# Paired PSUM tiles in the products and in-place column steps in a fused GEGLU and spectral-filter kernel

## The chip, the core and the metric

The kernel runs on one core of a Trainium2 chip. The metric is device microseconds (us) for one execution; the kernel before has a median of 1388.94 us over three runs (1387.86 to 1393.79).

The engines are named as the profile names them. PE is the matrix engine (PEld is its loading of weights), DVE the vector engine, ACT the scalar engine, POOL a fourth engine that here issues the DMAs that add into memory, and SP the engine that issues nearly all other DMAs. Each engine runs its own list of instructions strictly in the order in which the program wrote them. PSUM is the memory into which PE writes its sums, eight banks of 128 partitions by 512 numbers; SBUF is the memory from which the engines work. A program's buffers are *tiles*; the framework in which the kernel is written puts a semaphore wait in front of an instruction wherever a tile that it touches is still in use by another engine.

## The reference

```python
g = sigmoid((x * gate_w).sum(-1, keepdims=True))
a = irfft2(rfft2(x) * (w_r + 1j * w_i))          # over the 2048 x 576 plane
h = gelu_tanh(x @ w_gate) * (x @ w_up)           # 576 -> 4608
b = h @ w_down                                   # 4608 -> 576
out = g * a + (1 - g) * b                        # 2048 x 576, fp32
```

## The kernel before

**The GEGLU part** takes nearly all of PE's time. The 2048 tokens are four blocks of 512 (`TB`), the 4608 columns 36 tiles of 128. The first tiles are done directly (`chain`, L802). For the rest, two column tiles and two token blocks at a time are one *group* k, 0 to 33, and the four products of a group are made from seven by a Strassen–Winograd scheme (`products`, L1295). The seven products n = 0 to 6 carry the names a11, a12, s2, s3, s1, a22, s4. Each is made twice, once for the gate's columns (half s = 0) and once for the up-projection's (s = 1). A half is one call of `seven` (L1279): six matmuls of 128x512 (L1286) and one over 96 rows (L1288). Results pile up in PSUM. After n = 0 ACT copies each half into the accumulator of the other kind (`copy`, L235); after n = 2 and n = 3 it copies each half out to `xraw` in SBUF; after n = 4 and n = 6 DVE adds a half to what stands in `xraw` (`add`, L1328). Between the products stand eight calls of `down` a group (L891, twelve matmuls of 128x288), the down-projection of the group before. ACT moves each of their results to a staging tile (`stg<-pdn`, L923), and POOL adds it into memory by DMA (`yd<-stg`, L904).

PSUM before is split so that each half of a product has a tile of its own: `pgu` with two buffers, `px0` and `px1`, and `pdn` with two buffers of two banks each.

**The spectral part** (`spectral`) runs beside the groups: the rows' transforms, then 16 column steps (`columns`, L255) in which PE transforms blocks, DVE multiplies by the filter's weights and PE transforms back, then `inverse_tiles`, then the inverse of the rows in two parts (`inverse_rows`), which ends by adding its result into memory (`adds`). The column steps work on four groups of four tiles; a group needs a butterfly and twiddles (`four`, `tile_twiddles`) before its first step and again after its last. In between the operands of the second token half are made (`other_operands`) and, in group 15 (the *turn*), swapped in.

**The order of the work** is written out by the program. After each half product and each `down` comes a `gap`, in which the spectral part gets a credit of vector time that grows with PE's matmuls (RATE 1.08 against them) and writes pieces until the credit is spent. `at(n, f)` writes f some gaps later. STEP is the price of a column step in credit. So an instruction stands in its engine's queue where its gap put it, however late its inputs are. The queues of SP's DMAs have eight lanes; a DMA waits until its lane's previous one has landed.

## Time and profile before

| | |
|---|---|
| median of three runs | 1388.94 us (1387.86 to 1393.79) |
| the profiled execution | 1389.9 us, its span 1388.1 us |
| PE busy | 1330.7 us of the span, 7210 matmuls |
| DVE busy | 1150.5 us, 1814 instructions |
| ACT busy | 802.4 us, 1395 instructions |
| mean granted clock of PE | 0.983 |
| moved by DMA | 279.19 MB |

The span is what the profiler saw on the core, 1.8 us less than the execution. A page of the profile lists busy times; its slices cut the span into 40 equal pieces, where a digit is a tenth of the slice. The view of waits sums idle time of an engine by the instruction that ended it. The timeline lists instructions in order, with start and duration in us; a bracket gives the idle time just before and what released the engine. Successive matmuls overlap, so their starts are 0.23 us apart while each lasts 0.40. "x6" is six instructions in one row.

### The profile page before, as it was taken

How to read it: one execution, taken by the hardware profiler on the slowest of the kernel's cores; microseconds unless marked ns; L12 is line 12 of the kernel's file. 1: busy time of each engine (PE TensorE's matmuls, PEld its weight loads, DVE VectorE, ACT ScalarE, POOL GpSimd, SP SyncE). 2: the span in 40 equal slices, each digit the busy share in tenths (PEclk: the TensorE clock that was granted, in tenths of full speed). 3: DMA queues.
4: the chain of work that ended last, by engine and by line, in shares of the span. 5: the costliest groups of instructions: out<-in, count | busy, mean ns of one | idle time of the engine just before them, and what ended most of it. 6: DMA issues, size and time to landing. Idle time of an engine off the chain costs nothing. (4 is left out here: it accounts for less than half of the span.)

```text
span 1388.1 us, 21347 instructions
## 1 busy us (share of the span) xinstructions
PE 1330.7 (96%) x7210; PEld 1168.4 (84%) x7210; DVE 1150.5 (83%) x1814; ACT 802.4 (58%) x1395; POOL 274.8 (20%) x345
## 2 busy tenths in 40 slices
PE   9999999999999999796798989999999999999996
PEld 7878888888888888685787878888888888888896
DVE  7799999879989977664687787796999997899974
ACT  5575655655565556754575756665555556656541
POOL 0011111212111211111131122211211113311131
PEclk9999999999999999998899999999999999999999
DMA  9558888998877799899997979998877779977788
GB/s 345 197 138 181 175 182 175 236 260 188 183 135 135 135 248 306 239 254 291 253 265 191 263 164 256 247 270 233 172 134 135 133 134 207 180 141 132 129 181 222
DMA packets 184173, 279.19 MB, mean 201 GB/s; under 512 B 25920, under 2 KB 93568, under 8 KB 182144
## 3 DMA queue, kind: packets, MB, share of 16 engines
q0 software_dynamic: 47424, 91.51, 42.7%
q1 hardware_dynamic: 133184, 176.70, 40.5%
q10 hardware_dynamic: 3456, 9.62, 2.0%
q8 instruction: 57, 0.93, 0.3%
q14 instruction: 52, 0.43, 0.1%
HBM read 146.13 MB, written 129.20 MB: 198 GB/s over the span
## 5 line engine op out<-in xcount | busy, mean ns | idle before, releaser
L904 POOL DMA_DIRECT2D yd<-stg x264 | 228.4, 869 | 1044.4 <-ACT stg L923 973.3
L923 ACT ACTIVATE stg<-pdn,omg 128x576 f32<-128x576 f32 x276 | 204.3, 742 | 380.6 <-PE pdn L891 245.2
L891 PE MATMUL pdn<-dn,hb 128*128 128x288 f32 x1356 | 204.1, 298 | 13.0 <-ACT stg L923 12.9
L891 PEld LDWEIGHTS pdn<-dn,hb 128*128 128x128 f32 x1356 | 194.9, 190 | 23.4 <-ACT stg L923 14.9
L891 PE MATMUL pdn<-dn,ext 128*128 128x288 f32 x816 | 134.4, 301 | 22.4 <-ACT stg L923 14.3
L891 PEld LDWEIGHTS pdn<-dn,ext 128*128 128x128 f32 x816 | 125.6, 193 | 34.6 <-ACT stg L923 16.5
L1286 PE MATMUL pgu<-xhi,gub 128*128 128x512 f32 x480 | 152.5, 399 | 1.0 <-DVE gl L1311 1.0
L1286 PE MATMUL pgu<-til,gub 128*128 128x512 f32 x516 | 135.3, 398 | 7.0 <-ACT xraw L235 7.0
L891 PE MATMUL pdn<-dn,gub 128*128 128x288 f32 x816 | 132.2, 298 | 0.0
L235 ACT ACTIVATE gub<-low 128x512 fp32r<-128x512 f32 (+1 forms) x163 | 100.8, 620 | 31.3 <-DVE low L1257 17.6
L1286 PEld LDWEIGHTS pgu<-til,gub 128*128 128x128 f32 x516 | 96.3, 192 | 26.6 <-ACT xraw L235 7.6
L891 PEld LDWEIGHTS pdn<-dn,gub 128*128 128x128 f32 x816 | 118.1, 192 | 0.0
L1286 PE MATMUL px<-xhi,gub 128*128 128x512 f32 x344 | 107.6, 394 | 1.2 <-DVE xraw L1328 1.0
L1273 DVE TENSOR_TENSOR gub<-low,gub 128x512 fp32r<-128x512 f32 x151 | 103.4, 684 | 3.4 <-ACT gub L235 3.4
L1286 PEld LDWEIGHTS pgu<-xhi,gub 128*128 128x128 f32 x480 | 88.8, 192 | 16.9 <-DVE gl L1311 1.5
L1286 PE MATMUL px<-til,gub 128*128 128x512 f32 x396 | 101.8, 392 | 0.0
L1286 PE MATMUL pgu<-xlo,gub 128*128 128x512 f32 x240 | 94.7, 395 | 0.0
L1286 PEld LDWEIGHTS px<-til,gub 128*128 128x128 f32 x396 | 72.6, 188 | 14.0
L1286 PEld LDWEIGHTS px<-xhi,gub 128*128 128x128 f32 x344 | 62.2, 188 | 13.1 <-DVE xraw L1328 1.5
L891 PE MATMUL pdn<-dn,hx 128*128 128x288 f32 x444 | 70.7, 294 | 0.0
L93 DVE TENSOR_TENSOR rows<-rows 128x1280 f32<-128x1280 f32 (+1 forms) x57 | 69.5, 1219 | 0.8
L1288 PE MATMUL pgu<-til,gub 96*128 96x512 f32 x172 | 68.3, 397 | 0.3 <-DMA gub<-tails 0.3
(277 smaller groups left out, 2693.3 us busy)
## 6 DMA issues: line engine op xcount, KB each, us to landing
yd<-stg POOLq DMA_DIRECT2D x264, 288.0 KB, 5.1
low<-ws SPq DMA_DIRECT2D x114, 256.0 KB, 4.9
gub<-wd SPq DMA_DIRECT2D x68, 288.0 KB, 4.2
gub<-tails SPq DMA_DIRECT2D x537, 32.0 KB, 3.5
tails<-wtb SPq DMA_DIRECT2D x30, 448.0 KB, 4.8
wtb<-wf SPq DMA_DIRECT2D x32, 290.0 KB, 6.1
slot<-tails SPq DMA_DIRECT2D x177, 32.0 KB, 3.7
gub<-ws SPq DMA_DIRECT2D x22, 256.0 KB, 5.3
```

The costliest lines, as they stand in the source:

```text
L93: eng.tensor_tensor(o, p, q, op)
L235: act.activation(o, i, AF.Copy)
L891: pe.matmul(ps[half], h[:, l, c], d[:, q, half * HD:(half + 1) * HD], start=part == 0 and n == 0, stop=part == 1 and n == 2)
L904: pl.dma_start(yd[u], o, accum_op=ALU.add)
L923: at(n, lambda: put(u, lambda o: act.activation(o.rearrange("p (c k) -> p c k", c=2), v[:, :, 0:HD], AF.Copy, scale=omg[:, u:u + 1]), i == 0))
L1273: vec.tensor_tensor(v[:, 0:5:4], x, f(v[:, 1:4:2]), ALU.subtract)
L1286: pe.matmul(ps, l, x[:, t], start=first and t == 0 and q == 0, stop=False, skip_group_check=True)
L1288: pe.matmul(ps, w[0:96, 512 + P * s:512 + P * (s + 1)], xt[0:96], start=False, stop=True, skip_group_check=True)
```

## The change

1. **PSUM.** The two halves of a product become one tile of two banks (`ps_pair`, tiles `p0` and `p1`); `seven` writes `ps[:, s]`. ACT's copies are still made one half at a time, right after that half. DVE's `add` runs once on both halves (128x1024) instead of twice on 128x512, and the low parts of two down-weights are made by one operation of 2x576.
2. **Column steps.** Each group's four tiles stay in place in SBUF. The halves are swapped by the DMAs that load and store a tile (`corner`), so the DMAs between buffers (`bring`, `leave`) and the pass `inverse_tiles` are gone; the inverse's butterfly and twiddles run beside the steps (`forward`, `backward`, taken from `side`). Butterflies and twiddles become operations of 128x580 with the turn by 90 degrees on ACT (`turned`, two of 64x580). STEP is 8; a step takes its credit as it goes. The steps hold still during the turn (`hold`).
3. **Rows.** The passes before and after the column steps (`send_away`, `inverse_rows`) alternate between two places; some work moves between POOL, DVE and ACT; the result of the first part is added one gap apart rather than three.
4. **Starts.** The column steps begin while `other_operands` still runs (`go`), and two pieces of `tail_piece` a group are made in groups 1 to 4.

By count, PE's 7210 matmuls stay as they are. DVE goes from 1798 to 1674 vector operations, among them 544 for 680 of 128x512 and 68 of 128x1024 for none. ACT gets 84 of 64x580 for 32. SP's DMAs go from 1256 to 1202, their bytes from 278.8 to 263.9 MB.

```diff
-STEP = 6
+STEP = 8
...
-        def ps_gu():
-            return psum.tile([P, TB], F32, name="pgu", tag="pgu", bufs=2)
+        halves = {}
+
+        def ps_pair(n):
+            halves[n] = psum.tile([P, 2, TB], F32, name=f"p{n}", tag=f"p{n}", bufs=1)
+            return halves[n]
 
 ...
-        def ps_x(c):
-            return psum.tile([P, TB], F32, name=f"px{c}", tag=f"px{c}", bufs=1)
-
...
+        def turned(o, x, s):
+            act.activation(o[0:64], x[64:128], AF.Copy, scale=-s)
+            act.activation(o[64:128], x[0:64], AF.Copy, scale=s)
+        def column_four(T, at, tmps, sgn):
+            x0, x1, x2, x3 = (T[i] for i in at)
+            sp, y = tmps
+            for o, p, q, op in ((sp, x0, x2, ALU.add), (x0, x0, x2, ALU.subtract), (x2, x1, x3, ALU.add),
+                                (x1, x1, x3, ALU.subtract)):
+                vec.tensor_tensor(o, p, q, op)
+                yield 0.76
+            turned(y, x1, float(sgn))
+            for o, p, q, op in ((x1, sp, x2, ALU.subtract), (x2, sp, x2, ALU.add), (x3, x0, y, ALU.add),
+                                (x0, x0, y, ALU.subtract)):
+                vec.tensor_tensor(o, p, q, op)
+                yield 0.76
+        def column_twiddles(T, k, at, sgn, tmps):
+            def angle(o):
+                return sgn * math.pi * o * k / 8
+            for o in (1, 2):
+                turned(tmps[o % 2], T[at[o]], math.sin(angle(o)))
+            yield None
+            for o in range(1, 4):
+                x, t, c = T[at[o]], tmps[o % 2], math.cos(angle(o))
+                if o * k == 4:
+                    copy(x, t)
+                else:
+                    vec.scalar_tensor_tensor(x, x, c, t, op0=ALU.mult, op1=ALU.add)
+                    yield 0.77
+                if o == 1:
+                    turned(tmps[1], T[at[3]], math.sin(angle(3)))
...
+            def corner(o, x, out):
+
+                o = o.rearrange("p (c k) -> p c k", c=2)
+                for c in range(2):
+                    d, s = o[:, c].rearrange("(l m) k -> m l k", l=2), two(x)[64 * c:64 * c + 64]
+                    nc.sync.dma_start(*((d, s) if out else (s, d)))
+
+            def load_g(d):
+                for e in range(4):
+                    q = SW * (d + 4 * e)
+                    corner(away[:, q:q + SW], G[d % 2][e], False)
+
+            def store_g(d):
+                for e in range(4):
+                    q = SW * (d + 4 * e)
+                    corner(home[:, q:q + SW], G[d % 2][e], True)
 
...
+            made, done = [-1], [-1]
+            def forward(d):
+                if d:
+                    yield from column_twiddles(G[d % 2], d, TAKEN, -1, tmps)
+                yield from column_four(G[d % 2], TAKEN, tmps, -1)
+                made[0] = d
+            def backward(d):
+                while done[0] < 4 * d + 3:
+                    yield None
+                yield from column_four(G[d % 2], range(4), tmps, 1)
+                if d:
+                    yield from column_twiddles(G[d % 2], d, LEFT, 1, tmps)
+                at(2, lambda: store_g(d))
+                yield from waits(5)
+                if d < 2:
+                    load_g(d + 2)
+                    yield from waits(4)
+            def beside():
+                yield from forward(1)
+                for d in range(2):
+                    yield from backward(d)
+                    yield from forward(d + 2)
+                for d in range(2, 4):
+                    yield from backward(d)
...
+            side.append(beside())
+                while ops.get("hold"):
+                    yield None
...
+                    while made[0] < (kb + 1) // 4:
+                        credit[0] -= next(side[0]) or 0.0
+                    copy(xh, tile_of(kb + 1))
...
-                    n = count[0] + (1 + len(todo_t) % 2 if h else 3)
+                    n = count[0] + (1 + len(todo_t) % 2 if h else 1)
...
-            u, u3 = ([xraw[:, 2 * q + s] for s in range(2)] for q in range(2))
+            u, u3 = (xraw[:, 2 * q:2 * q + 2] for q in range(2))
...
             def add(o, v):
                 vec.tensor_tensor(o, o, v, ALU.add)
-                credit[0] -= 0.69
-
-            fore, acc = ([f() for f in fs] for fs in ((ps_gu, ps_gu), (lambda: ps_x(0), lambda: ps_x(1)))[::1 - 2 * (k % 2)])
+                credit[0] -= 1.22
+
-                if n in (4, 5):
-                    w, x = dn[(j + n - 4) % 4], b.wdr[n - 4]
-                    copy(w[:, 0], x)
-                    lower(("dn", j + n - 4), w, x, 0.76)
+                if n == 4:
+                    w, x = dns[:, j % 4:j % 4 + 2], b.both
+                    copy(w[:, :, 0], x)
+
+                    def rest_of(w=w, x=x):
+                        vec.tensor_tensor(w[:, :, 1], x, f(w[:, :, 0]), ALU.subtract)
+                        credit[0] -= 1.35
+
+                    seq(("dn", j), (5, rest_of))
...
-                    b.seven(ps[s], k, n, name, s, n in (0, 4), (lambda n=n, s=s: copy((acc, None, u)[n][s], ps[s])) if soon else None)
+                    b.seven(ps[:, s], k, n, name, s, n in (0, 4), (lambda n=n, s=s: copy((acc, None, u)[n][:, s], ps[:, s])) if soon else None)
                     if n in (0, 2, 3) and not soon:
-                        copy((acc, None, u, u3)[n][s], ps[s])
-                    elif n in (4, 6):
-                        at(0 if end else 1, lambda x=(u3, u)[n // 2 - 2][s], y=ps[s]: add(x, y))
+                        copy((acc, None, u, u3)[n][:, s], ps[:, s])
+                if n in (4, 6):
+                    at(0 if end else 1, lambda x=(u3, u)[n // 2 - 2], y=ps: add(x, y))
+                if turn and n == 1:
+                    ops["hold"] = True
...
+            if turn:
+                at(1, lambda: ops.pop("hold"))
```

**PE, the third product (n = 2) of group 25.** Names: `til`, `gub` and `slot` hold operands, `pgu` and `p_9425` are where the product goes, `pdn` is the next down-projection. L1286 and L1288 of before are L1319 and L1321 of the change. Before:

```order
L1286 MATMUL pgu<-til_305,gub_72 128x512 [waits DVE_49] x2
L1286 MATMUL pgu<-til_305,gub_72 128x512 x4
L1288 MATMUL pgu<-til_305,gub_72 128x512 [waits DMAHW4_49,DMAHW3_49,DMAHW2_49]
L1286 MATMUL pgu<-til_305,gub_72 128x512 x6
L1288 MATMUL pgu<-til_305,gub_72 128x512
L891 MATMUL pdn<-dn_75,ext 128x288 [waits Activation_49]
L891 MATMUL pdn<-dn_75,ext 128x288 x3
```

And now:

```order
L1319 MATMUL p_9425<-til_301,gub_72 128x512 [waits DVE_49] x2
L1319 MATMUL p_9425<-til_301,gub_72 128x512 x4
L1321 MATMUL p_9425<-til_301,gub_72 128x512 [waits DMAHW6_49,DMAHW5_49,DMAHW4_49]
L1319 MATMUL p_9425<-til_301,gub_72 128x512 [waits Activation_49]
L1319 MATMUL p_9425<-til_301,gub_72 128x512 x5
L1321 MATMUL p_9425<-til_301,gub_72 128x512
L921 MATMUL pdn<-dn,ext 128x288 [waits PE_49]
```

Each fence is one product: seven matmuls of half 0, then seven of half 1. Before, half 1 follows without a wait. Now its first matmul waits for ACT, whose copy of half 0 (`xraw<-p_9425`) is the instruction written between them; half 0 and half 1 are one tile. The same wait stands in the n = 0 and n = 3 products of all 34 groups, 102 in all, and at three places of `chain`.

**DVE, the start of the last group of column tiles.** L441 and L272 are twiddles, L93, L98 and L101 (now L251 and L256) the butterfly; L1328, L787, L1273 and L1311 (now L1362, L1377, L1306 and L1345) belong to the products. Before:

```order
L441 SCALAR_TENSOR_TENSOR rows<-rows,low 128x290
L1328 TENSOR_TENSOR xraw<-xraw,pgu 128x512 [waits PE_49]
L93 TENSOR_TENSOR gub_803<-rows 128x580 [waits DVE_49]
L93 TENSOR_TENSOR rows<-rows 128x580 [waits DVE_49]
L787 TENSOR_TENSOR dn_75<-gub_803,dn_75 128x576
L1328 TENSOR_TENSOR xraw<-xraw,pgu 128x512 [waits PE_49]
L1273 TENSOR_TENSOR gub_72<-low,gub_72 128x2x256 [waits DMAHW7_49,Activation_49]
L93 TENSOR_TENSOR rows<-rows 128x580 [waits DVE_49] x2
L98 TENSOR_TENSOR rows<-rows 128x290 [waits DVE_49]
L98 TENSOR_TENSOR rows<-rows 128x290
L1311 TENSOR_TENSOR xraw<-xraw 128x512 [waits Activation_49]
L787 TENSOR_TENSOR dn_76<-gub_803,dn_76 128x576 [waits DMAHW6_49]
```

And now:

```order
L402 TENSOR_TENSOR wtb<-gub_792,wtb 128x290 [waits DVE_49]
L1377 TENSOR_TENSOR dn<-gub_792,dn 128x2x576
L272 SCALAR_TENSOR_TENSOR rows<-rows,low 128x580 [waits DMAHW1_49,DMAHW0_49,Activation_49]
L272 SCALAR_TENSOR_TENSOR rows<-rows,low 128x580 [waits DMAHW5_49,DMAHW4_49,Activation_49]
L272 SCALAR_TENSOR_TENSOR rows<-rows,low 128x580 [waits DMAHW7_49,DMAHW6_49,Activation_49]
L251 TENSOR_TENSOR low<-rows 128x580 [waits DMAHW3_49,DMAHW2_49,DVE_49]
L251 TENSOR_TENSOR rows<-rows 128x580 [waits DVE_49] x3
L256 TENSOR_TENSOR rows<-low,rows 128x580 [waits DVE_49,Activation_49]
L256 TENSOR_TENSOR rows<-low,rows 128x580 [waits DVE_49]
L256 TENSOR_TENSOR rows<-rows,low 128x580
L256 TENSOR_TENSOR rows<-rows,low 128x580 [waits DVE_49]
L1345 TENSOR_TENSOR xraw<-xraw 128x512
```

What stood among the products' operations over many gaps now stands in one piece, eleven operations of 128x580 in a single gap.

**POOL, its last DMAs.** L904 (now L934) adds a down-projection's result, L652 (now L674) the spectral part's. Before, these are the last rows of the queue:

```order
L652 DMA yd_125<-gub_803 128x576 [waits DMASW2_49,DMASW1_49,DVE_49]
L904 DMA yd_124<-stg_88 128x576 [waits Activation_49]
L652 DMA yd_126<-wtb 128x576 [waits DMASW3_49,DVE_49]
L652 DMA yd_127<-low 128x576 [waits DMASW4_49,DVE_49]
L904 DMA yd_125<-stg_89 128x576 [waits DMASW5_49,DMASW1_49,Activation_49]
L904 DMA yd_126<-stg_90 128x576 [waits DMASW6_49,DMASW3_49,Activation_49]
L652 DMA yd_128<-tmp 128x576 [waits DMAHW7_49,DMASW7_49,DVE_49]
L652 DMA yd_129<-tmp 128x576 [waits DMASW0_49,DVE_49]
L652 DMA yd_130<-tmp 128x576 [waits DVE_49]
L652 DMA yd_123<-tmp 128x576 [waits DMASW2_49,DVE_49]
L652 DMA yd_124<-gub_803 128x576 [waits DVE_49]
```

And now, with nine more rows of L934 behind these:

```order
L674 DMA yd_120<-low 128x576 [waits DMASW1_49,DVE_49]
L674 DMA yd_121<-low 128x576 [waits DMASW2_49,DVE_49]
L934 DMA yd_124<-stg_85 128x576 [waits Activation_49]
L674 DMA yd_122<-tmp 128x576 [waits DMASW4_49,DMAHW7_49,DMASW3_49,DVE_49]
L674 DMA yd_123<-tmp 128x576 [waits DMASW7_49,DVE_49]
L934 DMA yd_125<-stg_86 128x576 [waits DMASW5_49,Activation_49]
L674 DMA yd_124<-tmp 128x576 [waits DMASW6_49,DMASW2_49,DVE_49]
L934 DMA yd_126<-stg_87 128x576 [waits Activation_49]
L934 DMA yd_119<-stg_84 128x576 [waits DMASW0_49,Activation_49]
L934 DMA yd_120<-stg_85 128x576 [waits DMASW1_49,Activation_49]
L934 DMA yd_121<-stg_86 128x576 [waits Activation_49]
```

The spectral part's last addition has moved from the end of the queue to ahead of the last rows of L934.

More of the change, by code (lines that the diff above doesn't have):

```diff
@@ L357, in columns @@
                 vec.tensor_tensor(vs2[:, 0], zr, zi, ALU.add)
                 vec.tensor_tensor(vs2[:, 1], zr, zi, ALU.subtract)
-                at(3, lambda kb=kb: load_ww(kb + 1))
-                if new:
-                    yield from group(new)
-                    bring(kb + 2)
+                at(2, lambda kb=kb: load_ww(kb + 1))
+                yield from step(0.91)
+                u = product(1, kb - 1, yh, yl) if was else None
                 yield from step()
                 if was:
-                    copy(two(out), u[:, :, :NK])
-                    at(1, lambda kb=kb: leave(kb - 1))
@@ L367, in columns @@
-                yield from step()
+                    copy(two(tile_of(kb - 1)), u[:, :, :NK])
+                    done[0] = kb - 1
+                yield from waits(STEP - 8)
             copy(yh, vs)
@@ L391, in inverse_tiles @@
+            done[0] = 15
+            yield None
+            for c in side.pop():
+                yield c
             yield from waits(2)
             set_tmp()
[L393 to L402 removed]
```

355 lines of the change are left out of this document (151 added, 204 removed).

## The prediction

> **What bounds the kernel now.** I read the page first, then the waits, then the time by stages. The page's busy times and slices:
>
> ```profile
> span 1388.1 us, 21347 instructions
> PE 1330.7 (96%) x7210; PEld 1168.4 (84%) x7210; DVE 1150.5 (83%) x1814; ACT 802.4 (58%) x1395; POOL 274.8 (20%) x345
> PE   9999999999999999796798989999999999999996
> PEclk9999999999999999998899999999999999999999
> ```
>
> PE is the bound: 57.4 us of idle time in 1388.1, in a few slices of the second half and in the last. Nothing that shortens DVE, ACT or DMA can win more than this idle time and the lower clock around it. The waits say who ends the large ones:
>
> ```profile
> PE pdn L891 <- ACT stg L923: 27.2, 9, 7.3
> PE pgu L1286 <- ACT xraw L235: 7.0, 1, 7.0
> PE pdn L891 <- DVE low L956: 8.0, 2, 7.1
> PE pgu L1286 <- ACT px L235: 2.5, 1, 2.5
> DVE low L956 <- DMA low<-yd: 7.5, 1, 7.5
> ```
>
> The first two and the fourth lie in the operands' stage, the turn and the column steps. The third is the end: the last down-projections wait for the results read back from memory. Windows of one quiet group and of the slices that lose time (columns: window, PE, PEld, DVE, ACT, POOL, clock, DMA share, GB/s):
>
> ```profile
> 1006.00:1041.30 35.30, 35.30 (x196) 31.19 (x195) 34.52 (x44) 20.07 (x36) 6.85 (x9) 1.00 0.74 133
> ...
> 555.20:589.90 34.70, 27.76 (x142) 23.29 (x141) 21.66 (x34) 27.47 (x48) 6.76 (x9) 0.95 0.87 238
> 624.60:659.30 34.70, 21.84 (x108) 18.44 (x107) 16.19 (x28) 16.76 (x30) 5.74 (x9) 0.89 0.95 291
> 659.30:694.00 34.70, 27.39 (x139) 24.50 (x138) 23.30 (x41) 17.46 (x31) 5.97 (x8) 0.82 0.95 254
> 728.70:763.40 34.70, 29.95 (x157) 26.45 (x157) 25.78 (x44) 18.66 (x34) 4.13 (x7) 0.90 0.73 191
> 798.10:832.80 34.70, 29.86 (x155) 26.57 (x155) 28.94 (x51) 20.75 (x37) 6.99 (x10) 0.90 0.78 165
> 1353.30:1388.00 34.70, 22.87 (x134) 21.00 (x132) 14.93 (x24) 5.19 (x9) 6.45 (x7) 0.90 0.90 223
> ```
>
> In the quiet group PE never idles, at full clock: 35.30 / 196 = 0.180 us a matmul. DVE is nearly as full (34.52). By that rate the five slices from 555 to 833 lost 34.70 less their matmuls at 0.180: 9.1 + 15.3 + 9.7 + 6.4 + 6.8 = 47 us, waits and lowered clock together.
>
> **The change part by part.** The sum is made against the profiled execution, 1389.9 us; the median of the runs is 1.0 below it.
>
> *The paired tiles.* In the order of the change, the first matmul of half 1 of products n = 0, 2 and 3 waits for ACT, and the only ACT instruction on its tile that is that new is the copy of half 0, which can't begin before the last matmul of half 0 has ended. These copies in the profile, by group of instructions:
>
> ```profile
> L235 ACT ACTIVATE xraw<-px 128x512 f32<-128x512 f32 x68 | 40.7, 599 | 17.1 <-PE px L1288 16.6
> L235 ACT ACTIVATE xraw<-pgu 128x512 f32<-128x512 f32 x68 | 40.5, 596 | 19.4 <-PE pgu L1288 14.5 <-DVE hb L876 4.0 <-DVE low L1257 0.3
> L235 ACT ACTIVATE px<-pgu 128x512 f32<-128x512 f32 x34 | 20.0, 588 | 4.6 <-PE pgu L1288 4.6
> L235 ACT ACTIVATE pgu<-px 128x512 f32<-128x512 f32 x34 | 19.9, 586 | 3.5 <-PE px L1288 3.5
> ```
>
> That is 204 copies of 0.60 us, half of them of half 0: 102 waits. Behind the waiting matmul stands everything that PE has left, so each costs PE time directly. Its price, from the timeline of PE and ACT:
>
> ```profile
> 1005.91 0.40 PE L1288 MATMUL pgu<-til,gub 96*128 96x512 f32 x1
> 1008.19 0.71 ACT L235 ACTIVATE px<-pgu 128x512 f32<-128x512 f32 x1
> 1020.36 0.40 PE L1288 MATMUL px<-til,slot 96*128 96x512 f32 x1
> 1020.79 0.60 ACT L235 ACTIVATE xraw<-px 128x512 f32<-128x512 f32 x1 [0.35 <-PE px L1288]
> 1041.22 0.40 PE L1288 MATMUL px<-til,slot 96*128 96x512 f32 x1
> 1041.45 0.63 PE L1286 MATMUL px<-xhi,slot 128*128 128x512 f32 x2
> 1041.78 0.59 ACT L235 ACTIVATE pgu<-px 128x512 f32<-128x512 f32 x1
> 1042.84 0.40 PE L1288 MATMUL px<-til,slot 96*128 96x512 f32 x1
> ...
> 561.76 0.73 PE L1286 MATMUL px<-xhi,gub 128*128 128x512 f32 x2 [1.03 <-DVE xraw L1328]
> 563.26 0.40 PE L1288 MATMUL px<-xtl,gub 96*128 96x512 f32 x1
> ...
> 579.04 0.57 ACT L235 ACTIVATE px<-pgu 128x512 f32<-128x512 f32 x1
> 579.67 1.22 PE L1286 MATMUL pgu<-xhi,slot 128*128 128x512 f32 x2 [2.50 <-ACT px L235]
> 582.39 0.63 PE L1288 MATMUL pgu<-til,slot 96*128 96x512 f32 x1
> ```
>
> Without a wait half 1 begins 0.23 us after half 0's last matmul began (1041.22 to 1041.45). With it: 0.40 until that matmul ends, 0.03 until a waiting ACT starts (1020.76 to 1020.79), 0.60 for the copy, 0.06 until PE resumes (579.61 to 579.67), 1.09 in all, or 0.86 more. After a wait of 1.03 us a half runs 0.11 longer (561.76 to 563.26 is 1.50, 1041.45 to 1042.84 is 1.39). The bounds are 0.86 and 0.97; between these I take 0.93, since the new wait is nearly as long as the one that shows the slow start. 102 x 0.93 = **+95** (88 to 99). The three of `chain`: **+3**.
>
> *ACT late for the copy.* Until now nobody waited for a copy that ACT made late. It starts 0.03 us after PE at 1020.79, 0.16 at 1041.78 (PE ended at 1041.62) and 1.88 at 1008.19 (1006.31). With the middle of the last two for n = 0 and 0.03 for the others a group has 1.08, 34 groups 37 us. But the pauses slow PE by 2.8 us a group while ACT's and DVE's other work stays, and so ACT catches up. I take 0.6 a group, **+21**, with ends 0 and 37.
>
> *The joint add* frees both halves at once. The next to write that tile is the product after next; a product and a `down` lie between, and hide it. Were they gone, n = 6 would wait too. DVE's shorter list is worth nothing by itself: no wait in the quiet group is DVE's.
>
> *Column steps, turn, operands.* At most the 47 us above can go. What stays? Butterfly operations:
>
> ```profile
> L93 DVE TENSOR_TENSOR tmp<-tmp 128x580 f32<-128x580 f32 x27 | 20.5, 760 | 0.7
> L346 ACT ACTIVATE rows<-rows 64x580 f32<-64x580 f32 x16 | 11.0, 688 | 0.2
> ```
>
> The order puts eleven of them in one gap before the last group of tiles: 11 x 0.76 = 8.4 us on DVE, with eight of 0.69 on ACT, while PE in a gap has about 1.6 us (1041.45 to 1043.07 by adding 0.23 to its last start). PE then waits for an eviction queued behind them, 7 us at worst, and gets a lower clock after. The turn keeps its seven swaps, now without column steps; before, it lost most of 15.3 + 9.7. I leave 15 of the 47 standing (ends 0 and 40, the latter where burst and turn cost as much as all stalls do now but one slice): **-32**. Evictions still queue behind `turned` on ACT, and that is what would be late next.
>
> *The end.* The spectral part's additions now precede the last of POOL's down-projection additions. Before:
>
> ```profile
> 1365.07 1.06 PE L891 MATMUL pdn<-dn,ext 128*128 128x288 f32 x6 [0.93 <-DVE low L956]
> 1373.12 0.82 DVE L956 SCALAR_TENSOR_TENSOR low<-pdn,omg,low 128x576 f32<-128x576 f32 x1 [7.51 <-DMA low<-yd]
> 1373.99 1.81 PE L891 MATMUL pdn<-dn,ext 128*128 128x288 f32 x6 [7.09 <-DVE low L956]
> ```
>
> The idle 8.0 us goes, and with the clock of 0.90 over 22.87 busy us in that slice 2.3 more: **-10** (0 to -10). The rest of the edits (row passes on two places, memsets, gates, tail pieces, fewer DMAs) lies in stretches where PE's slices read 9; PE's work hides them, and I take nothing for them. If that cover is gone they cost what their own stage's slack is short, which is in the ends above.
>
> Sum: 1389.9 + 95 + 3 + 21 - 32 - 10 = 1466.9, less 1.0 for the median: **1466 us**, own range 1435 to 1510. With every term at its lower end it would be 88 + 3 + 0 - 47 - 10 = +34, at its upper 99 + 3 + 37 - 7 + 0 = +132; the range leaves out the corners where all lie at one end.
>
> **The rivals.** *The pauses pay for the stalls* (0.08). For: in a group now lasting some 38 us DVE's 34.5 has room, so that no lateness and no stall is left, and the restart is free: the lower corner, 1389.9 + 34 - 1 = 1423. Against: the turn waits for transfers (DMA share 0.95 there).
>
> *The waits cost no PE time* (0.04, the other side). Place: the boundary between half 0 and half 1. If PE could have the next half's work under way during the copy, or a wait were met by the time PE gets there, only the gains would be left: 1389.9 - 32 - 10 = 1348. It decides below (47 + 10 - 3) / 102 = 0.53 us a wait; above that even the largest gain is used up. Against it speaks that the copy alone lasts 0.60 and starts only when PE has ended.
>
> *Cascade* (0.06). An ACT instruction that stands before a copy and waits for DVE or a DMA now stops PE at once, three times a group. The gain of 32 is lost again and the lateness goes to its end of 37: 1466 + 32 + 16 = 1514, and more where one such stop makes the next copy late.
>
> *The clock gives way* (0.04). After the wait of 2.50 us a half took 2.72 (579.67 to 582.39) against 1.39: 1.3 more. Were that so after each new wait, 102 x 1.3 = 133, about 1600. Against: after 1.03 us of idle time the half took 1.50. The new idle time is 0.03 + 0.60 + 0.06 = 0.69.
>
> The Trainium skill, "TensorE: Matmul & The Clock Gate", section "A second HAM failure mode: psum-queue depth-cycling", tells of a kernel in which PE idles briefly between groups of matmuls so often that its clock swings between half and full. By that rule the time would be this rival's; the trace shows only single waits, and after the short ones the clock held.
>
> **How the numbers follow.** The forecast has 0.78. What this kernel's measurement can tell from no change is about 0.5%, 7 us. Slower by more: 0.78 + 0.08 + 0.06 + 0.04 = 0.96, of which I give 0.01 to no change; of the other side's 0.04 faster has 0.03 and no change 0.01. So 0.03, 0.02, 0.95. The range 1410 to 1512 holds the forecast and the first rival; the other three, 0.14, lie outside.
>
> **What would show it.** In the profile after: about 102 waits of PE at half 1 for ACT's copies, 0.7 us each, some 70 to 90 us of idle time in all; a quiet group of about 38 us where it was 35.30; PE's busy time nearly as before and the clock at 1.00 there; no wait for DVE at the end; a stall at the eleven butterfly operations. It is wrong if the quiet groups still take 35.3 us, if the clock falls in them, or if PE waits at these places for something older than the copy.

## The result, and the profile after

The changed kernel takes 1516.74 us (median of four runs, 1514.22 to 1520.47). Against the kernel before, run beside it, the ratio is 1.0922, with a 95% interval from 1.0878 to 1.0966. It is slower, as forecast, and 51 us above the forecast of 1466, past the range's end at 1512. The profiled execution has a span of 1512.6 us, 124.5 more than before. The page's busy times and slices, after:

```profile
span 1512.6 us, 21107 instructions
PE 1362.7 (90%) x7210; PEld 1166.1 (77%) x7210; DVE 1139.4 (75%) x1682; ACT 844.8 (56%) x1419; POOL 271.5 (18%) x339
PE   9989898889999988888788779899999999999998
PEclk9999999999999999999899989999999999999999
```

The slices of PE have 8s from the third to the last, where before nearly all outside the middle read 9. A 9 stands for 90% or more and hides a part of the loss: the quiet group below has PE busy for 36.13 of 38.30 us, 94%, where it was 100%. The loss is everywhere, not in a stage alone. Of the 124.5 us, 32.0 are busy time of PE (1362.7 for 1330.7) and 92.5 idle time (149.9 for 57.4). The waits of PE, after:

```profile
PE p L1319 <- ACT xraw L228: 74.4, 68, 3.8
PE p L1319 <- ACT p L228: 47.3, 35, 11.1
PE pdn L921 <- ACT stg L953: 7.9, 1, 7.9
PE p L1321 <- DMA gub<-tails: 3.6, 1, 3.6
PE p L837 <- ACT gl L878: 2.9, 3, 1.4
```

The first two rows are the waits for ACT's copies of half 0: 103 times, 121.7 us. They were forecast as 102. The three of `chain` are there as well (L837). The waits for DVE at the end are gone. A quiet group in windows, and three of its waits in PE's timeline:

```profile
1379.30:1417.60 38.30, 36.13 (x195) 30.89 (x195) 32.60 (x52) 18.17 (x31) 6.82 (x8) 1.00 0.69 123
```

```profile
1379.05 0.73 PE L1319 MATMUL p<-xhi,gub 128*128 128x512 f32 x2 [0.79 <-ACT p L228]
1389.66 1.65 PE L1319 MATMUL p<-til,slot 128*128 128x512 f32 x6 [0.69 <-ACT xraw L228]
1395.44 1.65 PE L1319 MATMUL p<-til,gub 128*128 128x512 f32 x6 [0.69 <-ACT xraw L228]
```

The group lasts 38.30 us where it lasted 35.30: 3.00 for three waits. Of these 2.17 are idle and 0.83 are added busy time; the last section takes the latter apart. The granted clock is 1.00.

Not all waits are so short. Of the 103, 73 last 0.67 to 0.80 us, and the other 30 make up 69 us together. This is ACT and PE of the same kernel in group 2; a tail piece stands in ACT's queue before the copy:

```profile
160.62 0.59 ACT L1349 ACTIVATE gl<-p 128x512 f32<-128x512 f32 x1
162.53 0.95 ACT L228 ACTIVATE wtb<-wtb 128x896 fp32r<-128x896 f32 x1 [1.32 <-DVE wtb L1201]
163.38 0.58 ACT L228 ACTIVATE xraw<-p 128x512 f32<-128x512 f32 x1
```

```profile
161.17 0.40 PE L1321 MATMUL p<-til,gub 96*128 96x512 f32 x1
164.01 1.65 PE L1319 MATMUL p<-til,gub 128*128 128x512 f32 x6 [2.45 <-ACT xraw L228]
```

ACT first waits 1.32 us for DVE, then makes the tail piece, and only then the copy: PE stands for 2.45 us. The extreme is the turn, where ACT is held by its own swap of operands, since its queue issues these DMAs too (ACTq):

```profile
742.88 0.34 ACTq L1048 DMA_DIRECT2D xtl<-kept_s  x1
743.27 0.63 ACT L1349 ACTIVATE xraw<-xraw 128x512 f32<-128x512 f32 x1 [10.91 <-DMA gub<-tails]
745.01 1.22 PE L1319 MATMUL p<-xhi,gub 128*128 128x512 f32 x2 [11.15 <-ACT p L228]
```

The bracket names a DMA into `gub` as what ended ACT's idle time; but the last DMA of the swap stands ahead in ACT's queue, is issued at 742.88 and takes 0.34, and ACT goes on 0.05 us after that.

So the mechanism of the waits was the one forecast. What had to be found out was whether the waits alone make the loss, and where the forecast gain of 42 us (32 in the operands, the turn and the columns, 10 at the end) has gone.

### The profile page after: what moved, and what is told of

It reads as the page before. It is cut to its first block, busy times and chain, and to the rows that moved or that the text cites. A ratio compares the mean times of both kernels' runs of the same rounds, so it can differ in the third digit from the quotient of the medians.

```text
span 1512.6 us, 21107 instructions
## 1 busy us (share of the span) xinstructions
PE 1362.7 (90%) x7210; PEld 1166.1 (77%) x7210; DVE 1139.4 (75%) x1682; ACT 844.8 (56%) x1419; POOL 271.5 (18%) x339
## 4 chain that ended last, share of the span: by engine, by line
PE 73%; ACT 12%; DMA 8%; DVE 3%; issue 2%; SPq 1%; ACTq 0%; DVEq 0%
PE p L1319 36%; PE pdn L921 26%; PE p L1321 6%; ACT xraw L228 2%; ACT stg L953 2%; DMA gub<-tails 1%; DMA wtb<-wt 1%; PE pdn L326 1%; DMA rows<-away 1%; ACT p L228 1%; ACT xraw L1349 1%; PE p L857 1%; DMA til<-kept_s 1%; ACT ext L228 1%; SPq L296 1%
## 5 line engine op out<-in xcount | busy, mean ns | idle before, releaser
L934 POOL DMA_DIRECT2D yd<-stg x264 | 226.3, 858 | 1170.8 <-ACT stg L953 1110.9
L1319 PE MATMUL p<-xhi,gub 128*128 128x512 f32 x824 | 264.1, 402 | 39.2 <-ACT p L228 36.9
L1319 PE MATMUL p<-til,gub 128*128 128x512 f32 x912 | 244.1, 403 | 53.1 <-ACT xraw L228 53.1
L1319 PEld LDWEIGHTS p<-til,gub 128*128 128x128 f32 x912 | 164.8, 190 | 103.6 <-ACT xraw L228 74.5
L1319 PEld LDWEIGHTS p<-xhi,gub 128*128 128x128 f32 x824 | 148.5, 190 | 75.9 <-ACT p L228 48.0
L1319 PE MATMUL p<-xlo,gub 128*128 128x512 f32 x412 | 162.0, 393 | 0.0
L228 ACT ACTIVATE xraw<-p 128x512 f32<-128x512 f32 x136 | 81.3, 598 | 110.7 <-PE p L1321 106.5
L1362 DVE TENSOR_TENSOR xraw<-xraw,p 128x1024 f32<-128x1024 f32 x68 | 82.8, 1218 | 73.0 <-PE p L1321 72.9
L1321 PE MATMUL p<-til,gub 96*128 96x512 f32 x306 | 122.8, 401 | 3.6 <-DMA gub<-tails 3.6
L1306 DVE TENSOR_TENSOR gub<-low,gub 128x512 fp32r<-128x512 f32 x151 | 103.6, 686 | 18.1 <-ACT gub L228 17.9
L1319 PE MATMUL p<-til,slot 128*128 128x512 f32 x312 | 85.2, 410 | 21.3 <-ACT xraw L228 21.3
L1319 PE MATMUL p<-xhi,slot 128*128 128x512 f32 x264 | 84.7, 402 | 10.4 <-ACT p L228 10.4
L1319 PEld LDWEIGHTS p<-xlo,gub 128*128 128x128 f32 x412 | 78.4, 190 | 18.4
L1319 PEld LDWEIGHTS p<-til,slot 128*128 128x128 f32 x312 | 57.7, 195 | 39.8 <-ACT xraw L228 29.6
```

Source lines behind the costliest of these rows:

```text
L228: act.activation(o, i, AF.Copy)
L934: pl.dma_start(yd[u], o, accum_op=ALU.add)
L1306: vec.tensor_tensor(v[:, 0:5:4], x, f(v[:, 1:4:2]), ALU.subtract)
L1319: pe.matmul(ps, l, x[:, t], start=first and t == 0 and q == 0, stop=False, skip_group_check=True)
L1321: pe.matmul(ps, w[0:96, 512 + P * s:512 + P * (s + 1)], xt[0:96], start=False, stop=True, skip_group_check=True)
L1362: vec.tensor_tensor(o, o, v, ALU.add)
```

## The experiments

All kernels of this section compute the whole reference. A ratio is that to the kernel before, run beside it.

### The tiles: undone in the change, and done alone in the kernel before

`halves_apart` is the change with four PSUM tiles of one half each. `Apart` is a small class that holds two tiles and hands out the one of half s; the add becomes two again, at the same credit:

```diff
-            halves[n] = psum.tile([P, 2, TB], F32, name=f"p{n}", tag=f"p{n}", bufs=1)
+            if n in (0, 1):
+                halves[n] = Apart([psum.tile([P, TB], F32, name=f"p{n}{'ab'[c]}", tag=f"p{n}{'ab'[c]}", bufs=1) for c in range(2)])
...
-                vec.tensor_tensor(o, o, v, ALU.add)
+                if isinstance(v, Apart):
+                    for s in range(2):
+                        vec.tensor_tensor(o[:, s], o[:, s], v[:, s], ALU.add)
...
```

> The change with one thing undone: each half of a product has a PSUM tile of its own again, and the joint add is two adds of 128x512. Theory A (the shared tile makes half 1 wait for ACT's copy of half 0; that wait, ACT's lateness in it and the slow restarts are the whole loss, and the rest of the change is a gain): the 121.7 us of waits and about 30 us of PE's slower running go, some stalls that the pauses had covered come back: 1360 to 1385 us, faster than before by 0 to 2%. Theory B (much of the loss comes from the change's other parts, ACT's added turns and gate sums or the column steps in one piece, and would end in other waits if not in these): 1400 to 1450 us, slower than before.

It measured 1405.88 us, ratio 1.0141 (1.0115 to 1.0167). Of the 103 waits for copies 11 are left, 22 us together, and PE's busy time is that of before. The page's busy times, and PE's longest waits:

```profile
span 1404.2 us, 21211 instructions
PE 1329.2 (95%) x7210; PEld 1163.1 (83%) x7210; DVE 1139.1 (81%) x1750; ACT 842.2 (60%) x1419; POOL 272.1 (19%) x339
```

```profile
PE pdn L931 <- ACT stg L963: 19.0, 4, 16.6
PE p1a L1329 <- ACT p0a L238: 10.3, 2, 9.4
PE p1a L1331 <- DMA gub<-tails: 8.8, 1, 8.8
```

From 1.0922 to 1.0141 is a factor of 1.077, 108 us for the shared tiles. The two spans differ by 108.4 us as well, and their pages say what it is made of: 121.7 us of waits and 33.5 of PE's busy time (1362.7 to 1329.2) go, and 46.8 us of other waits come back, which the pauses had covered (28.2 to 75.0). But the time lies in theory B's range, at its lower end: what is left is slower than before by 1.4%, about 19 us, where theory A had a gain. The tiles are the larger part of the loss by far, and the rest of the change is a loss as well.

The halves of a shared tile lie in different banks. The Trainium skill, "PSUM — Partial Sum Buffer", section "PSUM bank collisions raise a hardware error", asks for semaphores by bank and quadrant, so that by its rule ACT may read one half while PE fills the other. In `halves_apart` PE goes on into half 1 while ACT copies half 0, and in its quiet groups, of 35.3 us, the 0.69 us at each of these places are gone. The wait of the change is the framework's, by tile, and not one that the chip needs.

`pairs_alone` is the kernel before with only the tiles shared:

```diff
+        def ps_half(n, c):
+            if c == 0:
+                pairs[n] = psum.tile([P, 2, TB], F32, name=f"p{n}", tag=f"p{n}", bufs=1)
+            return pairs[n][:, c]
...
-            return psum.tile([P, TB], F32, name="pgu", tag="pgu", bufs=2)
+            gus[0] += 1
+            return ps_half(1, (gus[0] + 1) % 2)
...
-            return psum.tile([P, TB], F32, name=f"px{c}", tag=f"px{c}", bufs=1)
+            return ps_half(0, c)
...
```

> The kernel before with one thing done: the two halves of a product share one PSUM tile; two adds, everything else as before. Theory A: 102 waits at 0.93 us and ACT's lateness of about 50 us on top of the kernel before, with none of the gains: 1389 + 95 + 50 = about 1530 us (1500 to 1550). Theory B (the lateness of ACT in the changed kernel comes from the work that the change put on ACT): 1389 + 95 + at most 20 = about 1490 to 1505 us.

It measured 1511.26 us, ratio 1.0898 (1.0865 to 1.0931), in theory A's range and near its lower end. Its waits for the copies:

```profile
PE p L1296 <- ACT xraw L245: 76.5, 69, 5.7
PE p L1296 <- ACT p L245: 33.1, 35, 2.5
```

That is 104 waits and 109.6 us, without any of the change's work on ACT. The shared tiles alone cost 125 us here. At 0.72 us each 104 waits would last 75 us, so 35 are lateness of ACT from the kernel's own work on it; the change has 48 (below).

`one_pair` leaves one of the two pairs shared, which keeps 51 of the 102 waits:

```diff
-            halves[n] = psum.tile([P, 2, TB], F32, name=f"p{n}", tag=f"p{n}", bufs=1)
+            if n in (0,):
+                halves[n] = Apart([psum.tile([P, TB], F32, name=f"p{n}{'ab'[c]}", tag=f"p{n}{'ab'[c]}", bufs=1) for c in range(2)])
+            else:
+                halves[n] = psum.tile([P, 2, TB], F32, name=f"p{n}", tag=f"p{n}", bufs=1)
```

> The change with the halves of tile p0 apart and those of p1 together: 51 of the 102 waits stay. Theory A (each wait has its own price): half way between the change and the version with all halves apart, about 1440 us (1430 to 1455). Rival (the loss is a cascade, in which one late copy makes the next late): much less than half the loss, below 1420 us.

It measured 1450.97 us, ratio 1.0472 (1.0443 to 1.0502). From 1.0141 the first 51 waits add 3.3% (46 us, 0.9 each), the next 51 another 4.5% (62 us, 1.2 each). It lies in theory A's range. The price is a third higher for the second 51, which are other places, and so not quite linear; a cascade that only sets in with all of them isn't there.

`joint_copy` keeps the shared tiles and copies both halves after half 1, behind which a down-projection stands:

```diff
...
-                    if n in (0, 2, 3) and not soon:
-                        copy((acc, None, u, u3)[n][:, s], ps[:, s])
+                if n in (0, 2, 3) and not soon:
+                    copy((acc, None, u, u3)[n], ps)
```

> The change with its shared tiles, but ACT copies both halves at once (128x1024) after half 1, for n = 0, 2 and 3; behind half 1 stands a down-projection of 1.6 us, and the copy takes an estimated 1.1 us. Theory A: PE has left half 0 and half 1 together, the copy is hidden by the down-projection where ACT is on time, and the time is that of the version with the halves apart plus what ACT is late by more than 0.4 us: 1365 to 1400 us. If the copy of twice the size comes out of the cover each time, 1400 to 1440 us.

It measured 1425.41 us, ratio 1.029 (1.0262 to 1.0319). That is past theory A's range and in that of the other case. The groups of its copies:

```profile
L228 ACT ACTIVATE xraw<-p 128x1024 f32<-128x1024 f32 x68 | 69.7, 1025 | 70.5 <-PE p L1321 70.4
L228 ACT ACTIVATE p<-p 128x1024 f32<-128x1024 f32 x34 | 34.4, 1011 | 19.1 <-PE p L1321 19.1
```

At 1.03 us the copy fits behind a down-projection of 1.6 us where ACT is on time, and then half 1 follows half 0 without a wait. Only 20 waits for copies are left, of 41 us together, so the copy doesn't come out of the cover each time, as the other case had it. Theory A's mechanism held; its range was built on 1360 to 1385 us for the halves apart, which took 1405.9. The shared tile costs far less if the copy's place in the order doesn't make PE wait. The version with halves apart, where a late copy holds up less (11 waits of 22 us), is 1.5% faster still.

### The rest of the change: why it is no gain

Where do the 19 us lie? Two windows hold the same work of PE in every kernel (their matmuls differ by one record at most): from the last matmul of the first half product of group 11 to that of group 24 (operands, turn and column steps are in it), and from that of group 33 to the end. First the kernel before, then `halves_apart`:

```profile
460.80:1005.90 545.10, 503.72 (x2715) 440.33 (x2714) 407.72 (x680) 332.72 (x584) 110.03 (x148) 0.97 0.92 238
1323.70:1388.10 64.40, 52.47 (x309) 47.93 (x307) 36.92 (x58) 19.73 (x33) 17.10 (x19) 0.95 0.88 193
```

```profile
461.70:1031.70 570.00, 504.97 (x2715) 440.15 (x2714) 421.56 (x656) 358.05 (x604) 109.22 (x145) 0.96 0.83 202
1349.80:1404.20 54.40, 50.08 (x309) 45.98 (x307) 21.25 (x32) 19.74 (x32) 9.37 (x11) 1.00 0.80 188
```

The end gives 10.0 us, the size forecast. The middle takes 24.9 us more, where it was forecast to take 32 less. All else of the two spans differs by 1.2 us.

In `halves_apart` the longest wait is 16.6 us, at the eleven butterfly operations that are written in one gap. ACT and PE there:

```profile
811.64 0.68 ACT L252 ACTIVATE low<-rows 64x580 f32<-64x580 f32 x1 [9.72 <-DMA rows<-away]
...
824.94 0.74 ACT L963 ACTIVATE stg<-pdn,omg 128x576 f32<-128x576 f32 x1
```

```profile
825.73 1.81 PE L931 MATMUL pdn<-dn,hb 128*128 128x288 f32 x6 [16.61 <-ACT stg L963]
```

The piece stands two gaps behind the load that it needs. ACT sits 9.72 us in front of its first turn until the load lands, and then does the turns, with DVE, until the eviction at 824.94 for which PE has been waiting. (In the change, where PE is later, the wait at this place is 7.9 us.) `apart_spread` lets the column steps wait until the piece has been written by credit, over ten gaps:

```diff
                     while made[0] < (kb + 1) // 4:
-                        credit[0] -= next(side[0]) or 0.0
+                        yield None
```

> The version with all halves apart (1405.9 us), and the last group's butterfly no longer written in one piece: the column steps wait until it has been written out by credit, over ten gaps, and ACT's turns are not at once behind the load that they need. Theory A (the piece stands behind a load that lands 9.7 us later on ACT, with the evictions behind it, and makes the 16.6 us wait of PE there): that wait and the slow clock after it go, 1380 to 1392 us. Rival (DVE and ACT are short of time in the column steps whatever the order): the wait goes elsewhere, 1398 to 1408 us.

It measured 1397.86 us, ratio 1.0089 (1.0062 to 1.0116). That wait is gone, but 7 us are won for its 16.6, and the intervals of the two ratios just touch; in the window of the middle it is 7.8 (570.0 to 562.2). The time lies between the two ranges, at the rival's edge. Waits of 3.9 and 3.2 us came up nearby. `pairs_spread`, the same edit in the change with its shared tiles, points the same way and lies in theory A's range, with intervals that overlap: 1508.49 us, ratio 1.0887 (1.0845 to 1.0929).

> The change as it is, shared tiles kept, with the last group's butterfly spread as in the first of these. Its wait was 7.9 us here, since PE was later by then. Theory A: 1500 to 1510 us. Rival (in the paused kernel the piece is covered): 1514 to 1518 us.

The next suspect was the loading of a group's tiles, which is eight DMAs for the four of before. In `apart_spread` SP is held by them while a product's operands are due:

```profile
547.42 9.56 SPq L306 DMA_DIRECT2D rows<-away  x8
557.37 1.72 SPq L1282 DMA_DIRECT2D gub<-wd  x2
```

```profile
569.38 0.77 PE L1331 MATMUL p1a<-til,gub 96*128 96x512 f32 x1 [7.49 <-DMA gub<-tails]
```

Three versions, all built on `apart_spread`, moved these loads: `apart_both` issues two DMAs a gap (stores too) and begins the second group's butterfly four gaps later, `apart_defer` loads the second group 9 to 15 gaps later, and `apart_spread_late` begins the column steps only when the operands are made. Their cores, in this order:

```diff
-                    corner(away[:, q:q + SW], G[d % 2][e], False)
+                    at(e if d else 0, lambda e=e, q=q: corner(away[:, q:q + SW], G[d % 2][e], False))
```

```diff
             def beside():
+                for e in range(4):
+                    q = SW * (1 + 4 * e)
+                    corner(away[:, q:q + SW], G[1][e], False)
+                    yield from waits(2)
+                yield from waits(3)
                 yield from forward(1)
...
-            load_g(1)
-            yield None
```

```diff
-                if i == 1:
-                    at(5, ops.pop("go"))
```

> As the one before, and the eight DMAs of a group's load or store are issued two a gap over four gaps, so that SP is not held for 8 us by them (the first load and last store stay as they are). Theory A: the wait of 8.8 us for a product's operands behind such a load goes too: 1370 to 1384 us, faster than the kernel before. Rival (the lanes are full anyway and the operands come as late): as the one before.

> The version with halves apart and the last butterfly spread (1397.9 us, ratio 1.0089), and the second group of column tiles is loaded 9 to 15 gaps later, one tile every second gap, not in the same stretch as the operands' stores. Theory A (SP is held there for 9.6 us by eight DMAs, the product's operands come late behind them, and PE waits 7.5 us for these): the wait goes, and what the lower clock costs after it: 1386 to 1391 us, ratio 1.001 to 1.005. Rival (the lanes and DMA engines are full there with the operands' own stores, as in the kernel before): same as without, 1395 to 1400 us.

> As the first of the two but the other way to part the two: the column steps begin only when the operands are made (some 6 gaps later), loads in one piece. Theory A: part of the wait of 7.5 us goes, 1390 to 1396 us. Rival: no change, 1395 to 1400 us.

They measured 1398.08 us (ratio 1.0101, 1.0069 to 1.0133), 1402.4 us (1.0106, 1.0071 to 1.0141) and 1398.09 us (1.0077, 1.005 to 1.0104): no gain in any. In `apart_both` the wait stayed (8.3 us), so spreading the load did not help the operands. In `apart_defer` it shrank to 1.7 as its theory had it, and part of the time came back at the turn, where 9.7 us became 14.1:

```profile
693.86 1.22 PE L1332 MATMUL p1a<-xhi,gub 128*128 128x512 f32 x2 [14.11 <-ACT p0a L238]
```

In `apart_spread_late` it is gone, and one of 9.0 us stands at a matmul of the column steps. Moving one late piece within this stage only moved the wait. The rivals were right here, in `apart_defer` with 2 us more than its range.

### The pace

The end's wait was gone in all versions of the change, as forecast, and yet the time as a whole showed no gain. `before_rate110` and `before_rate112` do this to the kernel before by one number, the credit of the spectral part:

```diff
-RATE = 1.08
+RATE = 1.10
```

> The kernel before with one number changed: the spectral part's credit is 1.10 of PE's time instead of 1.08, so that it ends 22 gaps before the last one rather than in it, and its DMAs are written ahead of the last down-projections'. Everything else is as before. Theory A (the last wait for the results read back, 8.0 us, and the clock after it come from the spectral part ending last, as the change removes it too): 1377 to 1382 us. Rival (what is gained at the end is paid in the stages before, which get denser): 1384 to 1392 us.

> The same with 1.12: the spectral part ends 43 gaps early. Theory A: the end's gain is had already with 1.10, and two hundredths more only make the stages denser: within 4 us of the version with 1.10. Rival (denser stages cost more than they did): 1386 to 1395 us.

They measured 1388.76 us, ratio 1.0015 (0.9992 to 1.0037), and 1398.6 us, ratio 1.0096 (1.0065 to 1.0126). Waits of PE with 1.10:

```profile
PE pdn L891 <- ACT stg L923: 16.9, 7, 6.8
PE pdn L307 <- ACT rows L235: 9.8, 1, 9.8
PE pdn L307 <- ACT gub L235: 6.4, 1, 6.4
```

The 8.0 us at the end are gone, and waits of 9.8 and 6.4 us that the kernel before doesn't have stand at the column steps. The same two windows with 1.10:

```profile
462.50:1017.10 554.60, 504.27 (x2715) 441.68 (x2714) 416.26 (x688) 336.72 (x587) 109.95 (x148) 0.96 0.91 234
1334.90:1389.20 54.30, 50.00 (x309) 45.92 (x307) 23.64 (x37) 19.49 (x33) 15.66 (x18) 0.99 0.94 236
```

The end gives 10.1 us, and the middle takes 9.5 more. So the rival was right with 1.10: the end's gain is paid in the stages before. With 1.12 neither guess held: the time is 3.6 us above even the rival's range. The second half's operands are made in gaps 318 to 350 of the kernel before, in 312 to 338 with 1.10 and in 301 to 327 with 1.12: 26 gaps for 32 in both. In the change they are made in gaps 294 to 320, as crowded, and its ratio with the halves apart and the butterfly spread, 1.0089, is near that of the kernel before with 1.12. The change asks for less credit in several places (1.22 for a joint add, where two adds asked 1.38), and that its spectral part runs ahead under the same number fits this, though no run took the credits apart. `apart_paced` gives it less up to the operands (the first line stands at two places) and more after:

```diff
+            rate[0] = 1.02
             yield from forward_rows()
...
+            rate[0] = 1.12
             yield from stage_two
```

> The version with halves apart and the last butterfly spread (ratio 1.0089), with the credit of the spectral part at 1.02 until the second half's operands are made and 1.12 from then on, in place of 1.08 throughout. The operands are then made in gaps 316 to 348, close to 318 to 350 of the kernel before, and not in 294 to 320; the spectral part ends 19 gaps before the last. Theory C (the change made the spectral part cheaper in credit, so it runs ahead and its operands' stage is crowded into 26 gaps where it had 32; the same crowding made the kernel before slower with a credit of 1.12): 1383 to 1391 us, ratio 0.998 to 1.004. Rival (the stage's work is what it is, and what is won in the operands comes back in the column steps): 1394 to 1402 us.

It measured 1374.33 us, ratio 0.9879 (0.9852 to 0.9906): 1.2% faster than the kernel before, and by more than theory C had. Windows of the operands' stage, the turn and the column steps (window, PE, PEld, DVE, ACT, POOL, clock, DMA share, GB/s), first of `apart_spread`, then of `apart_paced`:

```profile
495.00:605.00 110.00, 90.13 (x467) 76.45 (x466) 83.06 (x130) 76.44 (x130) 19.93 (x25) 0.95 0.93 234
605.00:710.00 105.00, 88.70 (x486) 77.53 (x485) 64.66 (x103) 62.13 (x108) 23.00 (x32) 0.95 0.98 256
710.00:910.00 200.00, 186.52 (x1004) 164.22 (x1004) 155.17 (x248) 136.02 (x229) 39.41 (x55) 0.96 0.75 176
```

```profile
530.00:620.00 90.00, 81.53 (x422) 70.37 (x421) 68.79 (x109) 67.65 (x115) 17.72 (x22) 0.94 1.03 266
620.00:725.00 105.00, 97.64 (x535) 85.31 (x534) 73.64 (x117) 65.98 (x114) 23.58 (x33) 0.98 0.91 238
725.00:925.00 200.00, 182.24 (x999) 161.22 (x998) 155.64 (x249) 139.56 (x236) 41.41 (x58) 0.97 0.81 191
```

The middle and the end of `apart_paced`, in the windows used above:

```profile
459.90:998.60 538.70, 502.56 (x2716) 440.37 (x2716) 401.54 (x637) 358.88 (x605) 109.64 (x145) 0.97 0.87 214
1318.00:1372.40 54.40, 50.07 (x309) 45.97 (x307) 24.71 (x38) 19.62 (x32) 17.88 (x19) 0.99 0.93 231
```

PE's idle time, window less busy time, goes from 19.9 to 8.5 us in the operands, from 16.3 to 7.4 at the turn, and from 13.5 to 17.8 in the column steps, where the credit is higher. The middle as a whole goes from 562.2 to 538.7 us, 6.4 less than in the kernel before, and the end keeps its 10.0; that is the gain of some 16 us. Three things stay open. The edit changes the length of the operands' stage, its distance from the turn and the pace behind it at once, so that crowding is the cause is likely and not shown. Which of the two new numbers does more, and what the pace does to the change with its shared tiles, wasn't run. And the kernel before was run only with one rate throughout; how much of the 1.2% it would win with two rates, without the change, isn't known.

## Why the prediction was right in its sign and wrong in its size

**The waits at half 1: right.** Their places and number are as forecast (102 and three; 103 and three in the trace). The price of 0.93 us was 1.00 in a quiet group (3.00 for three), just above the upper bound of 0.97. The shared tiles cost 108 us in the change and 125 in the kernel before; the forecast's three terms for them, 95 + 3 + 21, make 119. That this is so near is in part luck: the waits and PE's slower running came to 155 us (121.7 + 33.5), more than forecast, and the pauses won back 46.8 elsewhere, for which the sum has no term.

**ACT late for the copy: mis-sized.** I took 21 us, with an end at 37, since the pauses would let ACT catch up. The 103 waits last 121.7 us, and at 0.72 (2.17 / 3) they would last 74: 48 us of lateness. In the quiet group shown above ACT did catch up: no wait is more than 0.10 beyond 0.69. The step that failed is to take one lateness for all groups: it sits in 30 of the waits, where a copy is late by what stands before it in ACT's queue in that gap (2.45 us behind one tail piece). A part of the 48 is not the shared tiles': at the turn PE waits 9.4 us for a late copy with the halves apart too, for the 11.15 here.

**Operands, turn and column steps, -32: wrong.** This is the step that put the time out of the range. With the halves apart the middle takes 24.9 us more than before rather than 32 less (570.0 for 545.1), 57 us off, while the tiles came out 11 below their 119. At their upper ends the terms for the middle and the end still won 7 us; a loss was not allowed for. Two things failed. The first is the price of the eleven butterfly operations: I counted their work on DVE beyond a gap, 7 us at worst, and not that ACT would first wait 9.72 us for the load written two gaps ahead. In the change itself the wait is 7.9 us, near my bound, but with the halves apart PE stood for 16.6, and spreading them won 7.8 in the middle. The second is that I took the stages one by one, without asking where in the order the change had put them: under the same credit rate the operands came 24 gaps earlier and in 26 gaps instead of 32. Setting the pace was worth 23.5 us in the middle (562.2 to 538.7) and 2.1% in the time (1.0089 to 0.9879). Even then the middle wins 6.4 us and not 32. Which of the stalls that I took to go are bound to the work of these stages, whatever the order, no run shows. (I also put all nine waits of the first row, 27.2 us, into the middle; one of them, 1.86 us, stands at 76.90 us, at the start.)

**The end, -10: right.** From the first half product of group 33 the kernel before takes 64.4 us and the change with the halves apart 54.4. But the gain isn't the change's alone: a rate of 1.10 gives the kernel before the same 10.1 us there and costs it 9.5 in the middle, at a ratio of 1.0015. To sum the two terms as if they had nothing to do with each other was a part of the error.

**The rivals.** The waits cost PE time: `halves_apart` settles that. The pauses did pay for some stalls: PE's other waits are 28.2 us in the change and 75.0 without the pauses. It wasn't enough for that rival's 1423. The cascade gave 1514, within 3 us of the measured time, and part of its mechanism is there: an ACT instruction that waits for DVE or a DMA stops PE at once, and the lateness went past its end of 37. But its time is luck, since the gain that it lost was 32 and the middle was off by 57, and `one_pair` shows no cascade.

**The clock: it held at the short waits.** The mean granted clock is 0.978 for 0.983 before, and 1.00 in the quiet group with its three waits. The rule of the Trainium skill, "TensorE: Matmul & The Clock Gate", section "A second HAM failure mode: psum-queue depth-cycling", that short idle times between groups of matmuls make the clock swing, is not seen here at waits of 0.69 us three times in 38. At some of the long ones it did give way. Behind the wait of 2.45 us above, six matmuls took 1.65 us; in the same group, behind one of 3.08, they took 2.17, and the clock was 0.50 for a while:

```profile
172.19 2.17 PE L1319 MATMUL p<-til,gub 128*128 128x512 f32 x6 [3.08 <-ACT xraw L228]
```

```profile
173.20:176.50 3.30, 3.30 (x12) 2.92 (x12) 3.16 (x5) 0.87 (x3) 0.00 (x0) 0.50 0.54 171
```

By the mean clocks the change lost 33 us of clock (0.022 of 1512.6) and the kernel before 24 (0.017 of 1388.1), so this is a matter of 10 us and not of the rival's 133.

**DVE's shorter list: nothing by itself, as forecast.** DVE is 11 us less busy in the change, and the time followed PE's waits.

## What to carry to other kernels

Where one engine fills a buffer in halves and another empties them, look at what the waits are tied to: a tile that holds both halves makes the second fill wait for the first emptying, and that wait costs its whole length each time if the emptying stands directly between them in the order. Before a sum of a change's parts is believed, compare where its stages stand in the order before and after: work that became cheaper in a planner's credit runs ahead and can crowd a stage that was full already. And a wait that goes from one place is a gain only when the profile shows that it came up nowhere else.

## What the runs showed of the hardware

A wait of 0.69 to 0.79 us on PE costs about 1.00 us (3.00 for three a group). Six matmuls in a row in PE's timeline of the kernel before, to be held against the 1.65 us of the six after a wait, above:

```profile
1020.59 1.54 PE L1286 MATMUL px<-til,slot 128*128 128x512 f32 x6
```

They are 0.11 us slower after the wait, and the overlap of 0.17 us with the last matmul of half 0 (0.40 long, 0.23 to the next start) is lost; together that is the 0.28 us of added busy time a wait (0.83 for three). ACT's copy of 128x1024 out of PSUM takes 1.03 us, two of 128x512 take 1.20. The granted clock was 1.00 in a group with three waits of 0.69 to 0.79 us, and 0.50 for a while behind one of 3.08.
